# Activation, weight and table transposes of an SSM/MLP training step moved between the DMA queue and TensorE

## The chip, the core and the metric

One core of a Trainium2 chip runs the whole program: TensorE (PE) does the matmuls, VectorE (DVE), ScalarE (ACT) and GpSimd (POOL) the rest, and SyncE (SP) issues most of the DMAs. The metric is the device time of one execution in microseconds; lower is better. Engines run in parallel and each takes its own instructions in order, so an instruction that waits holds up everything behind it on its engine; the same is true of the transfers on one issuing queue.

## The reference, cut to what matters

The program computes a forward pass of four residual layers and the gradients of all their inputs. S = 2048 tokens, D = 512 features, F = 1376 hidden features, all in bf16.

```python
x = A_q
x = x + A(layernorm(x))      # A: q * (causal long convolution of kv with ssm_k + kv * ssm_D),
x = x + B(layernorm(x))      #    kv = shift_conv(k) * v
x = x + A(layernorm(x))
x = x + B(layernorm(x))      # B: gelu(x @ w1 + b1) @ w2 + b2
out, vjp = jax.vjp(f, A_q, A_k, A_v, A_shift_k, A_ssm_k, A_ssm_D, B_w1, B_b1, B_w2, B_b2)
return out, *vjp(grad_out)
```

The convolution's input does not depend on x, so it is done once (`y`) and both A layers use it. Backward, the gradient of y is the sum over both A layers (`gy_bf`), and one backward convolution follows. The weight gradients of w1 and w2 each sum over both B layers and all 2048 tokens: dw2 = h^T G, dw1 = (n^T gz), with h the gelu's output, G the gradient entering the layer, n the layer's normalised input and gz the gradient before the gelu. The gradient of b2 is the column sum of G over both layers.

## The kernel before

The program runs in stages. **Conv forward** (`phase_conv_forward`) makes sine tables (`tabN` for the filter, `tabF` and `tabI` for the data), shifts k, transforms filter and kv as matmuls over five frequency groups (`GROUPS`; `Fold.streams` prepares each group's input on DVE, `fwd_group` does the matmuls into `sp_ps`, `product` multiplies spectra on DVE, `inv_group` transforms back into `iv_ps`, `InvBlocks` combines on DVE). **MLP forward** and **MLP backward** (`phase_mlp`) cut the 2048 tokens into four slices of 512, each a lane (`fwd(s)`, `bwd(s)`); `interleave` emits the lanes in steps by a clock of rough costs, and the engines then run that order. A slice's input of a B layer is laid feature-major by DMA transposes on SP (`turn`, tiles `nT_sl` and, backward, `gT_sl`). The F features are handled as NFC = 11 chunks of 128 rows, the last with 96 rows and 32 of zeros. Backward, `b_bwd` needs w2 and w1 transposed (`w2T_sb`, `w1T_sb`); w1T has its mean over D removed (`centre_weights`, on DVE). h, gz and the gelu's derivative gp go to DRAM feature-major (`h_d`, `gz_d`, `gp_d`).

**Conv backward with weight gradients** is the last stage. `weight_grads` goes over 44 units (which weight, which layer, which chunk of 128 hidden features); a unit is 16 matmuls of 128x512 (`dw_ps<-G,dw_tm`), whose stationary operand `dw_tm` is h or gz with tokens on the partitions. That tile is fetched from `h_d` or `gz_d` by one DMA transpose on SP, five units ahead, in six buffers. The units' matmuls are the filler of the backward convolution: `conv_backward` yields numbers of microseconds at places where it expects PE to wait, and the top function puts that much filler there. PE's instructions are kept in that written order (`Ordered(nc, tc, ("tensor",))`); the other engines' orders are the scheduler's, by its own estimate of times. A finished sum goes from PSUM to SBUF on ACT (`dw_o`); for w1 it is also turned by four small matmuls (`dw_pt`, then `dw_oT` on ACT). Stores of results are issued on SP between the transposes (`flush`).

The backward convolution folds `gy_bf` on DVE (`fold_x`, `fold_s`, `fold_d`, `fold_t`), transforms it (`sp_ps` into `GY` on ACT), multiplies with the filter's spectrum (`Hb`, loaded on POOL's queue), transforms back, and makes the gradients of v, k and the shift filter. The filter's own gradient comes at the end (`cb_gh`): a table `tabG` of cosines and sines is built by POOL (`tg_u`), DVE and ACT, the spectra `GY` are multiplied in place with the data's spectrum (`KVb`, loaded on POOL's queue), and `gh_ps<-tabG,GY` are the last transforms.

The gradient of the output is loaded as `G` on SP at the end of the forward pass; out_0 and out_1 are stored half directly and half through a scratch copy in DRAM (`o0B`, `o1B`) that is reversed by `unflip_rows`.

## Time and profile before

| what | value |
|---|---|
| time, median of 3 runs (lowest to highest) | 1090.27 us (1090.2 to 1091.58) |
| profiled execution's own time | 1091.36 us |
| span of that execution in the profile | 1089.6 us |
| matmuls counted | 3856 |
| mean granted PE clock over the span | 0.87 of full speed |
| DMA traffic | 176.29 MB |

The profile gives, for one execution, how long each engine was busy, what ended its idle time, and which transfers were issued when. A matmul's own duration is its latency; matmuls follow one another faster than that, so the time of a row of n matmuls in the timeline, divided by n, is the cost of one. The granted clock scales it. Line numbers (L…) in rows of before are those of the listing above; L55 is a helper through which the ordered instructions go.

### The profile page before, as it was taken

The numbers are of one execution on the slowest core, as the hardware profiler recorded it, in microseconds if no ns is written. First come the engines' busy times: TensorE is split into PE (matmuls) and PEld (weight loads), VectorE is DVE, ScalarE is ACT, GpSimd is POOL, SyncE is SP. The second block draws the span as 40 slices with busy tenths as digits, with TensorE's granted clock in tenths as the row PEclk, the third lists the DMA queues.
The fourth block names the chain that finished last, engine by engine and source line by source line (L and its number), as shares of the span: only waits on it lengthen the run. The fifth ranks groups of instructions, "written<-read, shape, count | busy, mean of one in ns | idle before, by whom it ended". The sixth has DMA issues, their size and how long they took to land. (4 is left out here: it accounts for less than half of the span.)

```text
span 1089.6 us, 11131 instructions
## 1 busy us (share of the span) xinstructions
PE 785.0 (72%) x3856; PEld 359.2 (33%) x3917; DVE 728.8 (67%) x1373; ACT 468.8 (43%) x611; POOL 161.9 (15%) x281
## 2 busy tenths in 40 slices
...
GB/s 212 1 327 196 137 259 116 0 134 135 153 158 165 150 159 190 184 189 206 218 212 244 185 164 126 92 112 193 81 204 170 177 284 184 218 149 168 122 68 29
DMA packets 250979, 176.29 MB, mean 162 GB/s; under 512 B 152807, under 2 KB 238506, under 8 KB 250282
## 3 DMA queue, kind: packets, MB, share of 16 engines
...
q10 hardware_dynamic: 528, 0.00, 0.0%
...
## 5 line engine op out<-in xcount | busy, mean ns | idle before, releaser
L55 PE MATMUL dw_ps<-G,dw_tm 128*128 128x512 bf16 x687 | 171.5, 409 | 43.7 <-DMA dw_tm<-h_d 42.8
L957 PE MATMUL o_ps<-w_sb,h_sl 128*128 128x512 bf16 x345 | 96.0, 420 | 34.2 <-DVE h_sl L926 33.5
L55 PEld LDWEIGHTS <-dw_tm 128*128 128x128 bf16 x704 | 72.6, 105 | 135.5 <-DMA dw_tm<-h_d 41.5
L976 PE MATMUL gh_ps<-gT_sl,w2T_sb 128*128 128x512 bf16 x344 | 83.2, 390 | 29.6 <-DMA gT_sl<-G 26.6
L944 PE MATMUL z_ps<-nT_sl,w_sb 128*128 128x512 bf16 x345 | 82.6, 391 | 18.9 <-DMA nT_sl<-n_sl 18.1
L1032 ACT ACTIVATE nb_sl<-nb_sl,ab_ab 128x512 bf16<-128x512 bf16 x32 | 23.4, 802 | 159.4 <-DVE bb_junk L990 106.0
L987 PE MATMUL gn_ps<-w1T_sb,gz_sl 128*128 128x512 bf16 x345 | 83.3, 385 | 0.4
L1103 ACT ACTIVATE dw_o<-dw_ps 128x512 bf16<-128x512 f32 x22 | 13.1, 596 | 130.7 <-PE dw_ps L55 91.7
L978 DVE SCALAR_TENSOR_TENSOR gz_sl<-gh_ps,gpb 128x512 bf16<-128x512 f32 x88 | 58.5, 689 | 12.6 <-PE gh_ps L976 12.0
L946 ACT ACTIVATE g_z<-z_ps,b1col 128x512 bf16<-128x512 f32 x88 | 54.8, 694 | 19.9 <-PE z_ps L944 17.5
L957 PEld LDWEIGHTS <-h_sl 128*128 128x128 bf16 x352 | 34.0, 105 | 86.2 <-DVE h_sl L926 40.7
L976 PEld LDWEIGHTS <-w2T_sb 128*128 128x128 bf16 x352 | 35.1, 100 | 72.9 <-issue 34.8
L944 PEld LDWEIGHTS <-w_sb 128*128 128x128 bf16 x352 | 34.7, 100 | 64.7 <-DMA nT_sl<-n_sl 17.7
L987 PEld LDWEIGHTS <-gz_sl 128*128 128x128 bf16 x352 | 34.8, 99 | 40.7 <-issue 2.2
L869 POOL TENSOR_SCALAR rstd<-ln_mv 128x4 f32<-128x4 f32 x16 | 11.5, 719 | 236.2 <-DVE ln_mv L867 153.0
L922 ACT ACTIVATE g_s<-g_t 128x2048 bf16<-128x2048 bf16 (+1 forms) x24 | 42.5, 1773 | 8.9 <-DVE g_t L921 8.9
L993 POOL TENSOR_SCALAR bb_diag<-ident,bb_cols 128x128 bf16<-128x128 bf16 x32 | 17.0, 530 | 182.7 <-DVE bb_junk L990 181.8
L866 DVE BATCH_NORM_STATS2 ln_st<-x_sl 128x6 f32<-128x512 bf16 x64 | 41.9, 669 | 2.8 <-DMA x_sl<-in_A_q_dram 2.7
L919 ACT ACTIVATE g_q<-g_z 128x2048 bf16<-128x2048 bf16 (+1 forms) x24 | 42.9, 1788 | 0.1
L923 ACT ACTIVATE g_o<-g_t 128x2048 bf16<-128x2048 bf16 (+1 forms) x24 | 42.4, 1768 | 0.0
L880 ACT ACTIVATE n_sl<-x_sl,ln_nmr,rstd 128x512 bf16<-128x512 bf16 x32 | 24.7, 820 | 37.3 <-POOL ln_nmr L873 37.3
L55 PE MATMUL sp_ps<-fold_t,tabN 128*128 128x512 bf16 x85 | 30.2, 460 | 12.4 <-DVE fold_t L55 12.2
...
## 6 DMA issues: line engine op xcount, KB each, us to landing
n_d<-n_sl SPq DMA_DIRECT2D x16, 512.0 KB, 3.4
h_d<-h_sl SPq DMA_DIRECT2D x16, 512.0 KB, 2.9
gp_d<-g_p SPq DMA_DIRECT2D x16, 512.0 KB, 3.3
nb_sl<-n_d SPq DMA_DIRECT2D x16, 512.0 KB, 4.3
gpb<-gp_d SPq DMA_DIRECT2D x16, 512.0 KB, 5.0
gz_d<-gz_sl SPq DMA_DIRECT2D x16, 512.0 KB, 4.2
Hspec_d<-Hg SPq DMA_DIRECT2D x8, 512.0 KB, 4.1
...
```

The lines of the kernel that those rows point to most:

```text
L55: return self.tc.keep_in_program_order(f(*args, **kwargs))
L866: nc.vector.bn_stats(out=st, in_=x[:, t, :])
L880: nc.scalar.activation(out=n[:, t, :], in_=x[:, t, :], func=ACT.Identity, bias=nmr[:, t:t + 1], scale=rstd[:, t:t + 1])
L919: nc.scalar.activation(out=q, in_=zb, func=ACT.Square)
L922: nc.scalar.activation(out=sg, in_=t, func=ACT.Sigmoid)
L923: nc.scalar.activation(out=o, in_=t, func=ACT.Sigmoid, scale=-1.0)
L944: nc.tensor.matmul(ps, lhsT=w.w1[:, dc, c * P:(c + 1) * P], rhs=nT[:, dc, :], start=(dc == 0), stop=(dc == ND - 1))
L946: nc.scalar.activation(out=zb[:, c - c0, :], in_=ps, func=ACT.Identity, bias=w.b1col[:, c:c + 1])
L957: nc.tensor.matmul(ps, lhsT=h[:, c, t * P:(t + 1) * P], rhs=w.w2[:, c, :], start=False, stop=(c == NFC - 1))
L976: nc.tensor.matmul(ps, lhsT=w.w2T[:, dc, c * P:(c + 1) * P], rhs=gT[:, dc, :], start=(dc == 0), stop=(dc == ND - 1))
L978: nc.vector.scalar_tensor_tensor(out=gz[:, c, :], in0=ps, scalar=1.0, in1=gp[:, c - c0, :], op0=ALU.mult, op1=ALU.mult, accum_out=m.b1part ...
L987: nc.tensor.matmul(ps, lhsT=gz[:, c, t * P:(t + 1) * P], rhs=w.w1T[:, c, :], start=(c == 0), stop=(c == NFC - 1))
```

## The change

Seven edits, all in one step:

1. **Weight-gradient operands.** `dw_tm` is no longer fetched by a DMA transpose. A plain load on SP brings h or gz feature-major (`dw_fm`, four buffers, fetched four units ahead), 16 transposes on PE per unit turn it in two halves of eight into PSUM (`dw_tp`, two buffers), and ACT copies each half (128x1024) to `dw_tm` (three buffers). The halves of unit k+1 are placed after the matmuls 2 and 9 of unit k. The `dw_pt` matmuls of a finished w1 chunk move to matmul 5 of the next unit, the stores to matmul 12, and SP's order is kept as written for this part. `G` is reloaded in four pieces.
2. **Weights.** `w2T` and `w1T` are made on PE right after the forward convolution: 44 transposes and 8 copies for w2T; for w1T, 44 matmuls of 512 columns with a constant that subtracts the mean, 44 of 128 columns with the identity, and 11 copies on ACT. The DMA transposes and `centre_weights` go.
3. **The table of the filter's gradient.** `tabG` is turned out of `tabN` by 64 transposes on PE and 8 copies on ACT in the forward convolution, kept in DRAM (`tabG_d`) and loaded on POOL's queue where it was built before. Its 257th column is made apart (`col256`).
4. **b2.** The first of the 32 zero rows of the last chunk of w2 holds b2/16, and the bias of the matching hidden feature is 16, so that h there is 16: the matmul that added b2 (`o_ps<-b2row`) and the matmuls that summed G for its gradient (`db_ps`) go, and the gradient is a row of the last dw2 sum.
5. **Start of the backward pass.** `gT_sl` of the last layer is transposed straight from DRAM (grad_out and its flipped copy) and `G` and `nb_sl` are loaded after the slice's first group.
6. **Convolution backward.** `gy_bf` is left by the MLP backward already folded once (sums and differences of token pairs of a slice), so `fold_x` goes; `fold_d` is computed when group 2 asks for it. The product with `KVb` moves from the end into the loop over groups, behind `inv_group`. `unflip_rows` go on POOL's queue. `gk_o` shares buffers with `vb`.
7. **Pools** of these stages reuse memory tile by tile (`reuse_waits="tile"`): a new tile waits for the old tiles at its place, not for all of the closed pool.

SyncE at the end of the forward pass: x_sl is a slice's output, gpb the gelu's derivative loaded for the backward pass, gT_sl and G the incoming gradient. Before:

```order
L949 DMA h_d<-h_sl 128x3x512
L209 DMA out_dram<-x_sl 128x2x512
L950 DMA gp_d<-g_p 128x3x512
L55 DMA_TRANSPOSE w2T_sb<-w_sb 128x4x128
L209 DMA o0B_d<-x_sl 128x2x512
L55 DMA_TRANSPOSE w2T_sb<-w_sb 128x4x128
L55 DMA_TRANSPOSE w1T_sb<-w_sb 128x11x128 x4
L972 DMA gpb<-gp_d 128x4x512 x2
L211 DMA G_3677<-in_grad_out_dram 128x2x512
L211 DMA G_3677<-goB_d 128x2x512
```

After:

```order
L221 DMA out_dram<-x_sl 128x2x512
L926 DMA_TRANSPOSE gT_sl<-in_grad_out_dram 128x4x128 x2
L926 DMA_TRANSPOSE gT_sl<-goB_d 128x4x128 x2
L975 DMA h_d<-h_sl 128x4x512
L221 DMA o0B_d<-x_sl 128x2x512
L976 DMA gp_d<-g_p 128x4x512
L975 DMA h_d<-h_sl 128x3x512
L221 DMA out_dram<-x_sl 128x2x512
L976 DMA gp_d<-g_p 128x3x512
L221 DMA o0B_d<-x_sl 128x2x512
L995 DMA gpb<-gp_d 128x4x512
L223 DMA G_3864<-in_grad_out_dram 128x2x512
```

The transposes of the weights are gone from the queue, the transposes of gT_sl now read grad_out and its flipped copy and stand ahead of the last stores of the forward pass, and the loads of G follow the first gpb load instead of standing ahead of the first gT_sl.

SyncE at the end of the MLP backward and the start of the last stage: nb_sl holds the gradient of the first input here, o1B_d its half stored in scratch. Before:

```order
L1008 DMA nb_sl<-n_d 128x4x512
L209 DMA out_dram<-nb_sl 128x2x512
L209 DMA o1B_d<-nb_sl 128x2x512
L1065 DMA_TRANSPOSE dw_tm<-h_d 128x16x128 x2
L1186 DMA out_dram<-b1o 128x10x1
L1189 DMA out_dram<-b1o 96x1
L1065 DMA_TRANSPOSE dw_tm<-h_d 128x16x128
L209 DMA out_dram<-nb_sl 128x2x512
L209 DMA o1B_d<-nb_sl 128x2x512
L1065 DMA_TRANSPOSE dw_tm<-h_d 128x16x128
L199 DMA out_dram<-o1B_d 4x256x512
L1065 DMA_TRANSPOSE dw_tm<-h_d 128x16x128 x2
```

After:

```order
L221 DMA out_dram<-nb_sl 128x2x512
L221 DMA o1B_d<-nb_sl 128x2x512
L1100 DMA dw_fm<-h_d 128x2048
L55 DMA dw_fm<-h_d 128x2048
L1245 DMA out_dram<-b1o 128x10x1
L1248 DMA out_dram<-b1o 96x1
L55 DMA dw_fm<-h_d 128x2048
L221 DMA out_dram<-nb_sl 128x2x512
L221 DMA o1B_d<-nb_sl 128x2x512
L55 DMA dw_fm<-h_d 128x2048
L55 DMA out_dram<-dw_o 128x512
L55 DMA dw_fm<-h_d 128x2048 x2
```

Each fetch is now a plain load of 128x2048 instead of a transpose, six loads stand ahead of the last two nb_sl stores (three of them above this piece) where three transposes stood, and the reversal of o1B is not on this queue any more.

GpSimd at the end of the convolution's backward pass: tg_u are the arguments of the table, KVb the data's spectrum. Before:

```order
L690 DMA kTc<-kT_d 128x2176 x2
L685 DMA out_dram<-gk_o 128x4x512 x2
L738 DMA KVb<-KVspec_d 128x2x1024 x2
L711 IOTA qrow_i 128x272
L716 IOTA kcol_i 128x2 x2
L716 IOTA kcol_i 128x4 x3
L731 IOTA nyq_i 1x272
L713 CAST qrow<-qrow_i 128x272
L718 CAST kcol<-kcol_i 128x16
L723 TENSOR_SCALAR tg_u<-qrow,kcol 128x272 x12
L738 DMA KVb<-KVspec_d 128x2x2048
L723 TENSOR_SCALAR tg_u<-qrow,kcol 128x272 x8
```

After, the same place:

```order
L221 DMA o3B_d<-ksb_b 128x2x512
L211 DMA out_dram<-o3B_d 4x256x512
L713 DMA out_dram<-gk_o 128x4x512 x2
L718 DMA kTc<-kT_d 128x2176 x2
L713 DMA out_dram<-gk_o 128x4x512 x2
L739 DMA tabG<-tabG_d 128x16x256 x2
L740 COPY tabG<-col_80 128x32
L747 IOTA nyq_i 1x272
L791 DMA out_dram<-gh 128x2048 x4
L793 DMA out_dram<-gdo 128x4x1
```

The computation of tg_u is gone and two loads of the table stand in its place; the loads of KVb stand earlier, each behind the load of Hb of its group (not shown).

The diff, cut to its core:

```diff
-        unflip_rows(nc, aps["out_0"].flatten_outer_dims(), dram.o0B)
-        unflip_rows(nc, aps["out_1"].flatten_outer_dims(), dram.o1B)
...
-            nc = Ordered(nc, tc, ("tensor",))
-            fill = weight_grads(nc, m, dims, aps, dw)
+            conv_nc = Ordered(nc, tc, ("tensor",))
+            fill = weight_grads(Ordered(nc, tc, ("tensor", "sync")), m, dims, aps, dw)
...
 
 
+def turn_integer_table(nc, psum, pool, consts, tabN, dest):
+
+    for f in range(2):
+        for k0 in (0, 8):
+            tg = pool.tile([P, 8, 2, P], BF16, name="tg", tag="kn", bufs=4)
+            for qt in range(2):
+                ps = psum.tile([P, 8, P], BF16, name="tn_ps", tag="kt", bufs=2)
+                for k in range(8):
+                    nc.tensor.transpose(out=ps[:, k, :], in_=tabN[:, f, qt, (k0 + k) * P:(k0 + k + 1) * P],
+                                        identity=consts.ident)
+                nc.scalar.activation(out=tg[:, :, qt, :], in_=ps, func=ACT.Identity)
+            nc.gpsimd.dma_start(out=dest[:, f, k0:k0 + 8, :].rearrange("p k (t q) -> p k t q", t=2), in_=tg)
+
...
+        if k1 == 2:
+            tt(out=D, in0=X[:, :, 0:2], in1=X[:, :, 2:4], op=ALU.subtract)
...
+    turn_integer_table(nc, psum, gp, consts, tabN, dram.tabG)
...
-        gyv = res.gy_bf[:, :, :].rearrange("p (i h) d -> p i (h d)", i=4)
-        fg = Fold(nc, tp, gyv[:, :, 0:2 * D], gyv[:, :, 2 * D:4 * D], False)
-        yield 24.0
+        fg = Fold(nc, tp, None, None, False, res.gy_bf[:, :, :].rearrange("p (i e h) d -> p e i (h d)", i=4, e=2))
+        yield 28.0
...
+    unflip_rows(nc, aps["out_0"].flatten_outer_dims(), dram.o0B, eng=nc.gpsimd)
+    unflip_rows(nc, aps["out_1"].flatten_outer_dims(), dram.o1B, eng=nc.gpsimd)
...
                 inv_group(nc, psum, tabI, Y, g, W)
+                KV = gyp.tile([P, 2, 4, 512], BF16, name="KVb", tag="Sg", bufs=2)
+                dma(out=KV[:, :, 0:n, :], in_=dram.KVspec[:, :, base:base + n, :])
+                Rb = spec_second(nc, rot, KV) if g == 0 else None
+                product(nc, rot, GY[g], KV, Rb, g, GY[g], True)
+                yield 4.0
...
-                nc.vector.tensor_single_scalar(out=u, in_=u, scalar=8191, op=ALU.bitwise_and)
-                nc.scalar.activation(out=tabG[:, f, k0:k0 + 4, :], in_=u, func=ACT.Sin, scale=SIN_SCALE,
-                                     bias=consts.pibias)
+            dma(out=tabG[:, f, :, 0:256], in_=dram.tabG[:, f])
+        nc.gpsimd.tensor_copy(out=tabG[:, :, :, 256], in_=consts.col256)
...
-        for g, (k1, base, n) in enumerate(GROUPS):
-            KV = gyp.tile([P, 2, 4, 512], BF16, name="KVb", tag="Sg", bufs=2)
-            dma(out=KV[:, :, 0:n, :], in_=dram.KVspec[:, :, base:base + n, :])
-            Rb = spec_second(nc, hp, KV) if g == 0 else None
-            product(nc, hp, GY[g], KV, Rb, g, GY[g], True)
-            yield 1.3 * n
...
+    nc.gpsimd.memset(b1t[pad:pad + 1, nfull:nfull + 1], PAD_H)
+    nc.sync.dma_start(out=w.w2[pad:pad + 1, nfull, :], in_=aps["B_b2"].rearrange("(o d) -> o d", o=1))
+    nc.vector.tensor_scalar(out=w.w2[pad:pad + 1, nfull, :], in0=w.w2[pad:pad + 1, nfull, :], scalar1=1.0 / PAD_H,
+                            scalar2=None, op0=ALU.mult)
...
+    for dc in range(ND):
+        for c0 in (0, 8):
+            k = min(8, NFC - c0)
+            ps = psum.tile([P, 8, P], BF16, name="w2_ps", tag="mm", bufs=4)
+            for c in range(k):
+                nc.tensor.transpose(out=ps[:, c, :], in_=w.w2[:, c0 + c, dc * P:(dc + 1) * P], identity=consts.ident)
+            nc.scalar.activation(out=w.w2T[:, dc, c0 * P:(c0 + k) * P], in_=ps[:, 0:k, :], func=ACT.Identity)
     for c in range(NFC):
-        order.sync.dma_start_transpose(out=w.w2T[:, :, c * P:(c + 1) * P], in_=w.w2[:, c, :])
-        yield 8.0
...
+        ps = psum.tile([P, D], F32, name="w1_ps", tag="oo", bufs=4)
+        cs = slice(c * P, (c + 1) * P)
+        for dc in range(ND):
+            nc.tensor.matmul(ps, lhsT=w.w1[:, dc, cs], rhs=w.centre, start=(dc == 0), stop=(dc == ND - 1))
+        for dc in range(ND):
+            nc.tensor.matmul(ps[:, dc * P:(dc + 1) * P], lhsT=w.w1[:, dc, cs], rhs=consts.ident, start=False,
+                             stop=True, skip_group_check=True)
+        nc.scalar.activation(out=w.w1T[:, c, :], in_=ps, func=ACT.Identity)
...
-        nc.sync.dma_start_transpose(out=dst[:, :, t * P:(t + 1) * P], in_=src[:, t, :])
+        nc.sync.dma_start_transpose(out=dst[:, :, t * P:(t + 1) * P], in_=src[t])
...
-        nc.tensor.matmul(ps, lhsT=w.ones_row, rhs=w.b2row, start=False, stop=False)
...
+        if c0 == 0:
+            if load:
+                load()
+            n = m.spool.tile([P, TS, D], BF16, name="nb_sl", tag="n", bufs=m.n_bufs)
+            nc.sync.dma_start(out=n, in_=tok(m.n_d[l], s))
...
-        nc.vector.tensor_tensor(out=m.gy[:, sl, :], in0=m.gy[:, sl, :], in1=p, op=ALU.add)
+        nc.vector.tensor_tensor(out=p, in0=m.gy[:, sl, :], in1=p, op=ALU.add)
+        for e, op in enumerate((ALU.add, ALU.subtract)):
+            nc.vector.tensor_tensor(out=m.gy[:, s * TS + 2 * e:s * TS + 2 * e + 2, :], in0=p[:, 0:2, :], in1=p[:, 2:4, :],
+                                    op=op)
...
+    d.evp = stack.enter_context(tc.tile_pool(name="dw_ev", bufs=3, reuse_waits="tile"))
+    d.tp = stack.enter_context(tc.tile_pool(name="dw_tm", bufs=1, reuse_waits="tile"))
+    d.pp = stack.enter_context(tc.tile_pool(name="dw_ps", bufs=2, space=bass.MemoryType.PSUM, reuse_waits="tile"))
...
-    def fetch(k):
+    fms, tms, pss, turned, late = {}, {}, {}, [], []
+
+    def fetch(k, sync):
+        if k >= len(units):
+            return
         which, i, c = units[k]
-        tms[k] = d.tp.tile([P, NT, P], BF16, name="dw_tm", tag=f"dw_tm{i}")
-        nc.sync.dma_start_transpose(out=tms[k], in_=(m.gz_d if which else m.h_d)[layers[i]][:, c, :])
+        pool = d.evp if k % 4 == 3 else d.tp
+        fms[k] = pool.tile([P, S], BF16, name="dw_fm", tag=f"dw_fm{k % 4}", bufs=1)
+        sync.dma_start(out=fms[k], in_=(m.gz_d if which else m.h_d)[layers[i]][:, c, :])
+
+    def turn_half(k, half):
+        if k >= len(units):
+            return
+        if half == 0:
+            tms[k] = (d.evp if k % 3 == 2 else d.tp).tile([P, NT, P], BF16, name="dw_tm", tag=f"dw_tm{k % 3}", bufs=1)
+        ps = d.pp.tile([P, 8, P], BF16, name="dw_tp", tag="dw_tp")
+        for j in range(8):
+            t = 8 * half + j
+            nc.tensor.transpose(out=ps[:, j, :], in_=fms[k][:, t * P:(t + 1) * P], identity=m.ident)
+        dst = tms[k][:, 8 * half:8 * half + 8, :]
+        nc.scalar.activation(out=dst, in_=ps, func=ACT.Identity)
+
...
-    for k in range(ahead):
-        fetch(k)
-    psb = d.pp.tile([1, D], F32, name="db2_ps", tag="dw_ps")
-    for i in range(2):
-        for t in range(NT):
...
+    def reload(x, l):
+        for s in range(4):
+            nc.sync.dma_start(out=m.G[x][:, s * TS:(s + 1) * TS, :], in_=tok(m.n_d[l], s))
+
+    for k in range(4):
+        fetch(k, nc.nc.sync)
+    for half in range(2):
+        turn_half(0, half)
+        yield 0.45
     for k, (which, i, c) in enumerate(units):
-        if k + ahead < len(units):
-            fetch(k + ahead)
-        flush()
-        if which == 1 and (k == 0 or units[k - 1][0] == 0):
-            nc.sync.dma_start(out=m.G[1], in_=m.n_d[1].rearrange("(t p) d -> p t d", p=P))
+        if which == 1 and units[k - 1][0] == 0:
+            reload(1, 1)
+        fetch(k + 4, nc.sync)
         f0, fcs = dims.FC[c]
         if i == 0:
             pss[c] = d.pp.tile([P, D], F32, name="dw_ps", tag="dw_ps")
         ps, tm = pss[c], tms.pop(k)
         for t in range(NT):
+            if t in (2, 9):
+                turn_half(k + 1, int(t == 9))
+                yield 0.45
+            if t == 5:
+                turn_out()
+            if t == 12:
+                flush()
             nc.tensor.matmul(ps, lhsT=tm[:, t, :], rhs=m.G[i][:, t, :], start=(i == 0 and t == 0),
                              stop=(i == 1 and t == NT - 1))
             yield 0.23
...
+            turned.append((o, f0, fcs))
+    turn_out()
     flush()
...
+            turn_weights(nc, m.psum, m.w, wback, consts, dims)
...
+                g3 = G3[:, s * TS:(s + 1) * TS, :]
+                yield from b_bwd(nc, m, g3, 3, s, ret, dram_rows(go_ap, dram.goB, s),
+                                 lambda: tok_io(nc, g3, go_ap, dram.goB, s))
```

153 lines of the change are left out of this document (67 added, 86 removed).

## The prediction

> **What bounds the kernel now.** I first read the table of engine times by stage, cut where the work changes: conv forward, MLP forward, the passage to the backward pass, MLP backward, and the last stage in two pieces.
>
> ```profile
> core 0: us, PE busy (x) PEld busy (x) DVE busy (x) ACT busy (x) POOL busy (x), PEclk, DMA share, GB/s
> 0.00:220.00 220.00, 141.02 (x820) 69.70 (x829) 131.98 (x225) 103.25 (x134) 34.48 (x65) 0.84 0.43 155
> 220.00:480.00 260.00, 192.81 (x753) 74.86 (x768) 227.97 (x344) 211.63 (x224) 40.58 (x64) 0.87 0.54 161
> 480.00:506.00 26.00, 0.46 (x2) 0.14 (x2) 11.06 (x34) 6.46 (x10) 0.00 (x0) 0.60 1.03 252
> 506.00:698.00 192.00, 168.37 (x721) 70.98 (x735) 151.51 (x428) 37.33 (x52) 24.06 (x60) 0.96 0.64 180
> 698.00:760.00 62.00, 28.22 (x97) 10.51 (x98) 25.12 (x37) 4.87 (x8) 4.11 (x7) 0.69 0.75 134
> 760.00:1078.00 318.00, 254.10 (x1467) 133.03 (x1485) 181.14 (x307) 104.94 (x186) 58.67 (x85) 0.91 0.74 160
> ```
>
> No engine bounds the whole. DVE bounds MLP forward (228 of 260 us), PE MLP backward (168 of 192). In two places nothing computes: 480 to 506 and 698 to 760, and there the DMA share is highest (1.03 and 0.75). The last stage, 698 to 1078, is 380 us in which PE is busy 282. The list of waits of that stage says for whom:
>
> ```profile
> PE dw_ps L55 <- DMA dw_tm<-h_d: 42.8, 5, 15.7
> ACT dw_o L1103 <- DMA out_dram<-dw_o: 30.9, 2, 16.5
> PE dw_pt L55 <- ACT dw_o L1103: 27.4, 11, 9.2
> DVE fold_x L221 <- DMA o1B_d<-nb_sl: 23.8, 1, 23.8
> PE gt_ps L55 <- ACT gksT L670: 17.4, 8, 15.2
> ```
>
> PE's three rows make 42.8 + 27.4 + 17.4 = 87.6 us. The first is the transposed operand itself. The third begins with the second row: ACT stands 16.5 us at a dw_o whose buffer's store is not out, and the gksT copies behind it wait too. The timeline of PE and of SP's queue at the stage's start shows how:
>
> ```profile
> 714.78 4.91 PE L55 MATMUL dw_ps<-G,dw_tm 128*128 128x512 bf16 x22
> 735.44 9.98 PE L55 MATMUL dw_ps<-G,dw_tm 128*128 128x512 bf16 x31 [15.75 <-DMA dw_tm<-h_d]
> 759.17 3.41 PE L55 MATMUL dw_ps<-G,dw_tm 128*128 128x512 bf16 x9 [13.75 <-DMA dw_tm<-h_d]
> 762.42 1.89 PE L55 MATMUL sp_ps<-fold_t,tabFb 128*128 128x512 bf16 x8
> ...
> 712.57 10.27 SPq L1065 DMA_TRANSPOSE dw_tm<-h_d  x1
> 726.84 2.17 SPq L209 DMA_DIRECT2D o1B_d<-nb_sl  x1
> 737.57 21.33 SPq L1065 DMA_TRANSPOSE dw_tm<-h_d  x2
> ```
>
> One transpose holds SP for 10.27 us, two for 21.33. The o1B_d store comes behind the first, so its buffer is late for fold_x (the 23.8 us row), and sp_ps stands behind the dw_ps that wait. A matmul of 512 columns costs 4.91 / 22 = 0.223 us on a busy PE, but 9.98 / 31 = 0.322 after a wait: a long wait costs some 3 us more, as the granted clock (0.69 here, 0.91 later) confirms.
>
> **The change, part by part.** The sum is made against the profiled execution: 1091.36 us, of which the span is 1089.6; it lies 1.1 above the median of 1090.27.
>
> *Last stage.* The cost of transposes on PE comes from the ones before has in its prologue (three rows of PE's timeline, and the copies), and from 128-column matmuls that wait for nothing:
>
> ```profile
> 129.23 1.07 PE L55 MATMUL tt_ps<-ident,tabF 128*128 128x128 bf16 x16
> 134.75 1.93 PE L55 MATMUL tt_ps<-ident,tabF 128*128 128x128 bf16 x16 [4.45 <-ACT tabI L185]
> 136.87 3.72 PE L55 MATMUL tt_ps<-ident,tabF 128*128 128x128 bf16 x32 [0.20 <-ACT tabI L185]
> 926.66 9.10 PE L55 MATMUL gk_ps<-wdiag_b,gksT 128*128 128x128 bf16 x160
> ...
> L185 ACT ACTIVATE tabI<-tt_ps x4: 1017/1020/1024, 133.7 to 136.7; 128x1024 bf16<-128x1024 bf16 x4
> ...
> L55 PE MATMUL db_ps<-G,onescol x32: 379/379/634, 699.0 to 708.0; 128*1 128x512 bf16 x32
> ```
>
> 44 units x 16 = 704 transposes at 9.10 / 160 = 0.057 us are 40 us of PE; the upper bound is the prologue's pace, from 129.23 to 140.59, 11.36 / 64 = 0.178 us, 125 us in all. I take the lower one: between two halves lie seven matmuls of 0.223 us, 1.56 us, in which the 1.02 us copy fits, and there are two PSUM buffers. ACT gains 88 x 1.02 = 90 us; it was busy 110 of 380, and loses the table's sines. The db_ps go (some 9 us, 699.0 to 708.0). What the moves should buy is the waits: plain loads in place of transposes take away the 42.8 and the late stores behind them (15.2 of the 17.4, the 23.8 of fold_x, which itself is dropped). The dw_pt rows (27.4) go twice over: they move behind five matmuls of the next unit, and the table no longer puts ACT into POOL's pace. So of the 380: 380 - 88 = 292, less 9, plus 40, is 323 us. Less the slow matmuls after long waits, eight of them at 3.1, is 298. New waits come in: KVb shares its two buffers with Hb, so that each load starts later, and each half of PSUM waits for ACT. The next rows are for these, the loads in this stage and the two queues there (packets, MB, share of all DMA time):
>
> ```profile
> Hb<-Hspec_d POOLq DMA_DIRECT2D x3, 1024.0 KB, 14.2
> q1 hardware_dynamic: 106006, 32.09, 49.3%
> q0 software_dynamic: 7296, 26.89, 24.8%
> ```
>
> New waits are not in the trace: from 0 to the old 88. I take 20, one Hb landing of 14.2 and six for the rest, because the queue that carries the transposes (q1) pays 49.3 / 32.09 = 1.54% per MB against 0.92% on the other, so that Hb should land sooner than it did. Stage: 318, that is **-62** (-26 to -82).
>
> *Passage to the backward pass* (SP's queue, PE, DVE):
>
> ```profile
> 482.48 0.53 SPq L209 DMA_DIRECT2D o0B_d<-x_sl  x1
> 484.33 6.60 SPq L55 DMA_TRANSPOSE w1T_sb<-w_sb  x4
> 490.97 1.35 SPq L972 DMA_DIRECT2D gpb<-gp_d  x2
> 498.35 5.17 SPq L909 DMA_TRANSPOSE gT_sl<-G  x4
> 505.72 6.63 PE L976 MATMUL gh_ps<-gT_sl,w2T_sb 128*128 128x512 bf16 x21 [25.54 <-DMA gT_sl<-G]
> 507.62 0.69 DVE L978 SCALAR_TENSOR_TENSOR gz_sl<-gh_ps,gpb 128x512 bf16<-128x512 f32 x1 [4.01 <-PE gh_ps L976]
> ...
> gpb<-gp_d SPq DMA_DIRECT2D x16, 512.0 KB, 5.0
> ```
>
> w1T's transposes, G and gT_sl leave the chain; the last output's store stays ahead of gpb, so gpb is issued near 482.5 (where the last store is now), lands 5.0 later, and the first gz_sl comes near 487.5 instead of 507.6: **-20**. What is late next is gpb. Lower bound of the gain 12, if the eight gT_sl transposes that now stand ahead of the last stores hold SP for another 8 us (5.17 for four); upper 22.
>
> *MLP backward.* The pre-fold adds two half passes per slice. The nearest row is a whole pass:
>
> ```profile
> 701.13 1.22 DVE L1017 TENSOR_TENSOR ab_p<-nb_sl,g_sl 128x2048 bf16<-128x2048 bf16 x1
> ```
>
> Four slices at 1.22 to 2.44 are 5 to 10 us of DVE, beside a PE that is the bound; only the last slice's lies open: **+2** (0 to +10).
>
> *MLP forward and weights.* The 32 matmuls of b2row go, 32 x 0.223 = 7 us of PE in a stage that DVE bounds: **-3** (-7 to 0). The weights' 88 matmuls of 128 and 44 of 512 columns stand in an idle PE and ACT:
>
> ```profile
> 231.77 0.59 PE L954 MATMUL o_ps<-x_sl,ident 128*128 128x512 bf16 x1 [31.46 <-DVE x_sl L903]
> 237.12 2.93 ACT L880 ACTIVATE n_sl<-x_sl,ln_nmr,rstd 128x512 bf16<-128x512 bf16 x4 [35.70 <-POOL ln_nmr L873]
> 103.97 0.61 PE L55 MATMUL sp_ps<-fold_t,tabN 128*128 128x512 bf16 x1 [4.84 <-DVE fold_t L55]
> ```
>
> On a slow PE they take 88 x 0.116 (3.72 / 32) + 44 x 0.322 = 24 us, inside 31.46; ACT's 19 copies at most 19 us, inside 35.70: **0** (if the cover is gone, +24).
>
> *Conv forward.* 64 transposes are 7.4 us at that pace, and 4.84 of PE's wait at 103.97 covers most: **+3** (0 to +8).
>
> Sum: -62 - 20 + 2 - 3 + 0 + 3 = -80. Span 1010, execution 1011, median **1010**.
>
> **The rivals.**
>
> *Transfers stay late (1046).* The loads move as many bytes as the transposes did, over DMA engines that were busy 0.74 of the last stage, with POOL's 26.89 MB beside them. If half of the 88 us returns as waits for dw_fm, Hb and KVb, with half of the slow matmuls, the stage is 298 + 12 + 44 = 354: -26, sum -44. For it: POOL's queue gets two more loads and two reversals, and Hb took 14.2 us. Against: q1's price per MB, and SP held 10 to 21 us by transposes alone. [...] The two queue rows speak against it, though they hold other transfers too.
>
> *No new wait (985).* Stage 298, passage -22, prologue 0: -82 - 22 - 3 + 2 = -105. For it, a stretch of the stage that ran nearly so:
>
> ```profile
> 780.00:860.00 80.00, 75.63 (x333) 33.66 (x338) 51.09 (x72) 24.64 (x32) 8.66 (x13) 0.96 0.83 157
> ```
>
> Against: PE follows one written order, filled by guesses of how long the convolution waits.
>
> *The passage gains nothing (1030).* If the G loads or gpb behind them land as late as before, the -20 is lost. Against: gT_sl no longer reads G.
>
> *ACT sets PE's pace (1101, slower).* Place: each dw_tp half. If PE stands until ACT has copied, at the prologue's 1.42 us per eight (11.36 / 8) instead of 0.46, 88 halves cost 85 more, the clock stays low, and the stage is 323 + 85 = 408, +28; with -18 elsewhere +10. It decides from 75 / 88 = 0.85 us per half on. For it: ACT is in order, and its row of 30.9 shows that it can stand. Against: the prologue's last 32 took 0.93 per eight with nothing between the halves. [...]
>
> **How the numbers follow.** Forecast 0.50, late transfers 0.24, no new wait 0.13, no gain in the passage 0.06, ACT's pace 0.07. From 978 to 1052 lie nearly all of the first and fourth, four fifths of the second and half of the third: 0.8. The forecast's own range is 995 to 1028. About 0.2% (2 us) is what a measurement can tell from no change: faster 0.91, same 0.03 (the upper end of late transfers), slower 0.06.
>
> **What would show it.** Right: PE's wait for its first gh_ps under 8 us and the first gz_sl near 487; no wait of dw_ps for a transfer over 5 us; sp_ps starting under 40 us after the last MLP backward matmuls instead of 64 (762.42 less 698); the last stage some 318 us at a clock of 0.95. Wrong: dw_tp waiting for ACT in total over 30 us; product rows waiting for Hb or KVb; gh_ps waiting for tabG; w1T's matmuls pushing the first z_ps past 246.

## The result and the profile after

The changed kernel takes 1017.74 us (four executions, 1014.58 to 1019.7) against 1090.92 us of the kernel before, run beside it (four, 1090.2 to 1093.6): a ratio of 0.9322, 95% interval 0.9293 to 0.9351. Measured again later it took 1022.32 us (six, 1018.95 to 1024.64), ratio 0.9367 (0.9329 to 0.9404), so two measurements of one kernel can lie 0.5% apart. Ratios leave out executions that lie over 1.5% above the fastest of their kernel, which matters below for two of the kernels with transposing loads; differences between kernels of different chips are therefore taken from the ratios.

First the table of engine times by stage, cut where the work changes (the first three rows are the forward pass and the passage to the backward pass, the fourth the MLP backward, the last two the last stage up to the convolution's first transform and from there):

```profile
core 0: us, PE busy (x) PEld busy (x) DVE busy (x) ACT busy (x) POOL busy (x), PEclk, DMA share, GB/s
0.00:208.00 208.00, 143.49 (x880) 74.81 (x890) 113.70 (x191) 109.01 (x140) 37.74 (x90) 0.87 0.48 174
208.00:254.00 46.00, 19.98 (x141) 11.04 (x142) 38.26 (x79) 15.95 (x26) 5.14 (x12) 0.73 0.30 87
254.00:489.70 235.70, 181.19 (x733) 75.90 (x747) 209.70 (x301) 209.55 (x222) 35.95 (x52) 0.90 0.56 163
489.70:688.50 198.80, 164.08 (x707) 69.81 (x722) 153.70 (x432) 42.41 (x59) 30.83 (x61) 0.95 0.69 197
688.50:731.00 42.50, 30.98 (x204) 17.03 (x205) 22.47 (x38) 18.75 (x22) 6.64 (x9) 0.90 0.70 184
731.00:1009.00 278.00, 263.14 (x2016) 159.35 (x2049) 171.08 (x299) 167.79 (x252) 33.72 (x47) 1.00 0.59 187
```

In the last stage (688.5 to 1009) PE is busy 31.0 + 263.1 = 294.1 of 320.5 us, at a full clock from 731 on. Before it was busy 28.2 + 254.1 = 282.3 of 380. So the stage has 11.8 us more of PE's work and 97.7 - 26.4 = 71.3 us less idle time: -59.5. For the comparison the stages are cut at these rows of the timeline, the last matmuls of the conv forward, of the MLP forward and of the MLP backward. Before (the row of the first gz_sl stands in the prediction):

```profile
195.83 4.48 PE L55 MATMUL iv_ps<-Yg,tabI 128*128 128x512 bf16 x20
477.42 2.76 PE L957 MATMUL o_ps<-w_sb,h_sl 128*128 128x512 bf16 x12 [0.76 <-DVE h_sl L926]
696.20 1.71 PE L995 MATMUL gn_ps<-nb_sl,bb_diag 128*128 128x512 bf16 x3 [6.27 <-DVE bb_junk L990]
1077.77 0.60 ACT L1111 ACTIVATE dw_oT<-dw_pt 128x512 bf16<-128x512 f32 x1 [0.54 <-PE dw_pt L55]
```

And after, with the first gz_sl, the first sp_ps of the last stage and the last store of the convolution:

```profile
203.31 5.87 PE L55 MATMUL iv_ps<-Yg,tabI 128*128 128x512 bf16 x22 [0.22 <-issue]
485.89 2.76 PE L982 MATMUL o_ps<-w_sb,h_sl 128*128 128x512 bf16 x12 [0.30 <-DVE h_sl L952]
494.53 0.69 DVE L1001 SCALAR_TENSOR_TENSOR gz_sl<-gh_ps,gpb 128x512 bf16<-128x512 f32 x1 [5.34 <-DMA gpb<-gp_d]
686.81 1.72 PE L1023 MATMUL gn_ps<-nb_sl,bb_diag 128*128 128x512 bf16 x3 [7.00 <-DVE bb_junk L1018]
731.33 1.90 PE L55 MATMUL sp_ps<-fold_t,tabFb 128*128 128x512 bf16 x8 [2.03 <-DMA tabFb<-tabF_d]
977.22 0.76 POOL L793 DMA_DIRECT2D out_dram<-gdo  x1
1008.96 0.60 ACT L1120 ACTIVATE dw_oT<-dw_pt 128x512 bf16<-128x512 f32 x1 [0.49 <-PE dw_pt L55]
```

Start plus duration of these rows gives the end of each stage (for the first gz_sl its start counts). Forecast and measured differences:

| stage, ending at | before, us | after, us | difference | forecast |
|---|---|---|---|---|
| conv forward, last iv_ps | 200.3 | 209.2 | +8.9 | +3 |
| MLP forward with the weights, last o_ps | 279.9 | 279.5 | -0.4 | -3 |
| passage, first gz_sl | 27.4 | 5.9 | -21.5 | -20 |
| MLP backward, last gn_ps | 190.3 | 194.0 | +3.7 | +2 |
| last stage, last dw_oT | 380.5 | 321.0 | -59.5 | -62 |
| tail, end of the span | 11.2 | 3.2 | -8.0 | none |
| span | 1089.6 | 1012.8 | -76.8 | -80 |

The waits of the last stage, in which before's rows began with 42.8 for dw_tm:

```profile
ACT dw_tm L1112 <- PE dw_tp L55: 70.4, 74, 7.1
PE dw_tp L55 <- DMA dw_fm<-h_d: 7.8, 2, 6.1
PE gt_ps L55 <- ACT gksT L698: 3.6, 8, 1.2
PE dw_ps L55 <- ACT dw_tm L1112: 1.9, 3, 1.2
```

ACT waits for PE's transposes 70 us, PE for ACT's copies 1.9 us in all. The groups of the stage's transposes and copies:

```profile
L55 PE MATMUL dw_tp<-ident,dw_fm 128*128 128x128 bf16 x704 | 55.2, 223 | 7.8 <-DMA dw_fm<-h_d 7.8
L1112 ACT ACTIVATE dw_tm<-dw_tp 128x1024 bf16<-128x1024 bf16 x88 | 89.8, 1023 | 74.8 <-PE dw_tp L55 70.4 <-DVE bb_junk L1049 4.0 <-remote 0.3
```

The queues (packets, MB, share of all DMA time) and the loads (KB each, us to land):

```profile
q1 hardware_dynamic: 19986, 29.47, 34.2%
q0 software_dynamic: 8880, 30.04, 26.5%
Hb<-Hspec_d POOLq DMA_DIRECT2D x3, 1024.0 KB, 5.6
tabFb<-tabF_d POOLq DMA_DIRECT2D x1, 2048.0 KB, 24.2
out_dram<-o1B_d POOLq DMA_DIRECT2D x1, 1024.0 KB, 23.3
```

SP's queue moves 29.47 MB in 19,986 packets where it was 32.09 MB in 106,006, and a megabyte costs 34.2 / 29.47 = 1.16% of the stage's DMA time instead of 1.54%. As the windows differ in length (319 and 380 us), that is 3.7 us of all 16 DMA engines for a megabyte instead of 5.8. Hb lands in 5.6 us instead of 14.2, but tabFb in 24.2 where it took 11.1 before.

### The profile page after: what moved, and what is told of

Its sections match the earlier page's. It is cut to its first block, busy times and chain, and to the rows that moved or that the text cites. A ratio compares the mean times of both kernels' runs of the same rounds, so it can differ in the third digit from the quotient of the medians.

```text
span 1012.8 us, 12851 instructions
## 1 busy us (share of the span) xinstructions
PE 802.9 (79%) x4675; PEld 408.0 (40%) x4753; DVE 708.9 (70%) x1337; ACT 564.0 (56%) x718; POOL 150.0 (15%) x271
## 4 chain that ended last, share of the span: by engine, by line
PE 22%; DVE 21%; DMA 13%; ACT 9%; issue 7%; POOL 4%; SPq 2%; POOLq 0%; DVEq 0%; another core or an unknown queue 0%; ACTq 0%
PE dw_ps L55 7%; PE gh_ps L999 4%; DVE ln_st L883 2%; DMA tabFb<-tabF_d 2%; DMA gpb<-gp_d 2%; PE gh_ps L55 2%; PE sp_ps L55 2%; DMA nb_sl<-n_d 2%; PE dw_tp L55 2%; DVE g_o L953 2%; DMA ksb_b<-ks_d 2%; ACT g_o L949 2%; ACT g_z L972 2%; ACT g_s L948 2%; DVE gz_sl L1001 2%
## 5 line engine op out<-in xcount | busy, mean ns | idle before, releaser
L55 PE MATMUL dw_ps<-G,dw_tm 128*128 128x512 bf16 x671 | 166.3, 383 | 3.5 <-ACT dw_tm L1112 1.9
L1112 ACT ACTIVATE dw_tm<-dw_tp 128x1024 bf16<-128x1024 bf16 x88 | 89.8, 1023 | 74.8 <-PE dw_tp L55 70.4
L55 PEld LDWEIGHTS <-dw_tm 128*128 128x128 bf16 x704 | 65.3, 99 | 63.1 <-ACT dw_tm L1112 3.0
L1015 PE MATMUL gn_ps<-w1T_sb,gz_sl 128*128 128x512 bf16 x344 | 80.6, 379 | 1.3 <-DVE g_sl L1024 0.9
L1001 DVE SCALAR_TENSOR_TENSOR gz_sl<-gh_ps,gpb 128x512 bf16<-128x512 f32 x88 | 58.2, 688 | 25.6 <-DMA gpb<-gp_d 16.1
L982 PEld LDWEIGHTS <-h_sl 128*128 128x128 bf16 x352 | 36.5, 107 | 93.0 <-DVE h_sl L952 45.1
L55 PE MATMUL dw_tp<-ident,dw_fm 128*128 128x128 bf16 x704 | 55.2, 223 | 7.8 <-DMA dw_fm<-h_d 7.8
L55 PEld LDWEIGHTS <-dw_fm 128*128 128x128 bf16 x704 | 48.0, 100 | 29.3 <-DMA dw_fm<-h_d 8.7
L999 PEld LDWEIGHTS <-w2T_sb 128*128 128x128 bf16 x352 | 35.3, 101 | 59.5 <-issue 21.2
L945 ACT ACTIVATE g_q<-g_z 128x2048 bf16<-128x2048 bf16 (+1 forms) x24 | 42.8, 1783 | 0.1
L1039 ACT ACTIVATE ab_u<-y_res,onescol_f,rstd 128x512 bf16<-128x512 bf16 x32 | 23.3, 802 | 29.4 <-DVE G L1062 22.9
```

The source lines that it names most:

```text
L55: return self.tc.keep_in_program_order(f(*args, **kwargs))
L945: nc.scalar.activation(out=q, in_=zb, func=ACT.Square)
L982: nc.tensor.matmul(ps, lhsT=h[:, c, t * P:(t + 1) * P], rhs=w.w2[:, c, :], start=False, stop=(c == NFC - 1))
L999: nc.tensor.matmul(ps, lhsT=w.w2T[:, dc, c * P:(c + 1) * P], rhs=gT[:, dc, :], start=(dc == 0), stop=(dc == ND - 1))
L1001: nc.vector.scalar_tensor_tensor(out=gz[:, c, :], in0=ps, scalar=1.0, in1=gp[:, c - c0, :], op0=ALU.mult, op1=ALU.mult, accum_out=m.b1part ...
L1015: nc.tensor.matmul(ps, lhsT=gz[:, c, t * P:(t + 1) * P], rhs=w.w1T[:, c, :], start=(c == 0), stop=(c == NFC - 1))
```

## The experiments

Edit numbers are those of the section on the change; all kernels but the second are edits of the changed kernel.

**Edit 1 undone: transposing loads again, everything else kept.** The operand comes from a DMA transpose, six buffers, five units ahead.

```diff
-        fms[k] = pool.tile([P, S], BF16, name="dw_fm", tag=f"dw_fm{k % 4}", bufs=1)
-        sync.dma_start(out=fms[k], in_=(m.gz_d if which else m.h_d)[layers[i]][:, c, :])
+        tms[k] = pool.tile([P, NT, P], BF16, name="dw_tm", tag=f"dw_tm{k % 6}", bufs=1)
+        sync.dma_start_transpose(out=tms[k], in_=(m.gz_d if which else m.h_d)[layers[i]][:, c, :])
...
-                turn_half(k + 1, int(t == 9))
```

> The changed kernel (1017.7 us), with only the way of the weight-gradient operand put back: dw_tm comes by DMA transposes on SP again, five units ahead in six buffers; no transposes and no copies of it on PE and ACT. All other edits stay. My theory is that the transposes' delay was what the last stage lost: of PE's old waits the 42.8 us for dw_tm and the 15.2 us behind late dw_o stores return, and 40 us of PE transposes go, but PE then idles in their place; the last stage, 321 us now, becomes 340 to 355, the whole 1035 to 1050. Rival: the other edits of that stage (dw_pt moved, table loaded, product moved, pools, reversals off SP) brought the gain, and the PE transposes only cost their 40 us; then the stage falls to about 285 and the whole to 980.

Measured: 1064.15 us, ratio 0.973 (0.9684 to 0.9775). That is 0.036 to 0.041 above the change, 40 to 44 us: above the theory's range, and far from the rival's. The kernel has 704 transposes and 88 copies less and is slower. How much of this belongs to the reversals, which the change puts beside these loads, is asked further below.

**Edit 1 alone, put into the kernel before.** Plain loads, transposes on PE, moved dw_pt and SP's written order for this part, in the old pools' places (dw_ev with two buffers, for room; the three pools of the weight gradients reuse memory tile by tile, so a part of edit 7 comes along).

```diff
-        nc.sync.dma_start_transpose(out=tms[k], in_=(m.gz_d if which else m.h_d)[layers[i]][:, c, :])
+        fms[k] = pool.tile([P, S], BF16, name="dw_fm", tag=f"dw_fm{k % 4}", bufs=1)
+        sync.dma_start(out=fms[k], in_=(m.gz_d if which else m.h_d)[layers[i]][:, c, :])
...
+                turn_half(k + 1, int(t == 9))
```

> The kernel before (1090.9 us) with only the way of the weight-gradient operand changed: plain loads, transposes on PE, copies on ACT, dw_pt behind five matmuls of the next unit, stores behind twelve, SP's order as written there. The sums for b2's gradient, the table built by POOL, the order of products and the pools of the convolution stay as before. My theory: waits of 42.8 + 15.2 us and the 23.8 us of fold_x go, 40 us of PE come, so some 40 to 50 us are won, 1040 to 1050. Rival, that this edit needs the others (the table's sines in ACT's order hold up the copies, the reversals hold up SP): below 15 us won, 1075 or more.

Measured: 1067.27 us, ratio 0.978 (0.9742 to 0.9819), 24 us faster than before; between the two expectations, so both missed. Its last stage is 363.8 us, 16.7 less than before; its tail is 3.2 us instead of 11.2. The waits in its last stage:

```profile
DVE fold_x L221 <- DMA dw_fm<-h_d: 18.5, 1, 18.5
PE dw_ps L55 <- ACT dw_tm L1081: 17.1, 4, 7.8
ACT tabG L726 <- DVE tg_u L725: 14.9, 7, 4.0
PE dw_tp L55 <- DMA dw_fm<-h_d: 10.3, 2, 6.3
```

PE's waits for the operand's transfers fall from 42.8 us to 10.3, and waits for ACT's copies come in: 15.5 of these 17.1 us lie between 890 and 960, where ACT makes the table and waits for DVE. So ACT stands there in the table's pace, set by POOL and DVE; fold_x still waits behind the stage's loads. The operand is worth 24 us alone and 40 to 44 with the other edits, the reversals on POOL's queue among them.

**Edit 3 undone: the table built by POOL, DVE and ACT at the end** (no turning in the conv forward; gh with two buffers, for room).

```diff
-    turn_integer_table(nc, psum, gp, consts, tabN, dram.tabG)
...
-            dma(out=tabG[:, f, :, 0:256], in_=dram.tabG[:, f])
+            for k0 in range(0, 16, 4):
+                u = hp.tile([P, 4, NQP], I32, name="tg_u", tag="tg_u", bufs=2)
```

> The changed kernel with only the table of the filter's gradient put back: built by POOL, DVE and ACT in the last stage, and not turned out of tabN in the forward convolution (the filter gradient's result tiles have two buffers instead of four, to make room). In the trace of the change the forward convolution ends 8.9 us later than before and the 64 transposes stand in it from 99.5 to 108.8 where before had a gap of 4.8. If that edit costs the prologue its time and the chain at the end has slack (the filter's gradient is done 32 us before the end), this is 4 to 8 us faster, 1010 to 1014. Rival: POOL's 26 us chain puts ACT and with it the dw_tm copies behind it, PE stalls for 10 to 20 us in the last stage, and this is slower, 1022 to 1032.

Measured: 1027.21 us, ratio 0.9397 (0.9355 to 0.944); this is the rival's range, not the expected gain. By the ratios it is 3 to 8 us slower than the two measurements of the change, and its interval overlaps that of the second. The profile, of the longest of the four executions, splits it: the last stage is 338.2 us (+17.2), the conv forward ends at 206.0 (-3.2). Two of PE's waits in the last stage:

```profile
PE gh_ps L55 <- ACT tabG L748: 5.3, 1, 5.3
PE dw_tp L55 <- ACT dw_tm L1121: 4.2, 1, 4.2
```

The table on ACT delays both the last transforms and the operand's copies. These rows are 9.5 of the 17.2 us; the rest is open.

**The operand turned twice.** Each half is transposed and copied twice, so the same result costs 704 transposes and 88 copies more; the filler that a half counts for is doubled with it.

```diff
+        ps = d.pp.tile([P, 8, P], BF16, name="dw_tp", tag="dw_tp")
+        for j in range(8):
+            t = 8 * half + j
+            nc.tensor.transpose(out=ps[:, j, :], in_=fms[k][:, t * P:(t + 1) * P], identity=m.ident)
+        nc.scalar.activation(out=dst, in_=ps, func=ACT.Identity)
```

> The changed kernel with every half unit of the weight-gradient operand turned and copied twice, into the same place: 704 more transposes on PE (40 us at 0.057) and 88 more copies on ACT (90 us at 1.02). If a transpose costs only its own PE time, as the sum took it, the whole is 40 to 46 us longer, 1058 to 1064. Rival: ACT's copies set PE's pace (two PSUM buffers now serve twice the halves); then a second copy costs its own 1.02 us and the whole is 75 to 95 us longer, 1093 to 1113.

Measured: 1065.35 us, ratio 0.977 (0.9735 to 0.9804), just above the theory's range and far from the rival's. The last stage is 370.7 us, 49.7 longer: 49.7 / 704 = 0.071 us per transpose, copies and waits included, 0.56 per half. ACT as the pace, 1.02 us per half, would have cost 90. Both copies in its last stage, and what ACT waits for:

```profile
L1112 ACT ACTIVATE dw_tm<-dw_tp 128x1024 bf16<-128x1024 bf16 x88 | 90.1, 1024 | 36.3 <-PE dw_tp L55 33.2 <-remote 2.9
L1117 ACT ACTIVATE dw_tm<-dw_tp 128x1024 bf16<-128x1024 bf16 x88 | 90.1, 1023 | 2.9 <-PE dw_tp L55 0.2
```

Even with twice the copies ACT stands 33 us waiting for PE.

**Edit 5 undone: gT from G.** G is loaded ahead of the backward pass and gT_sl transposed out of it.

```diff
+        for i in range(NSL):
+            tok_io(nc, G3[:, i * TS:(i + 1) * TS, :], go_ap, dram.goB, i)
...
-                yield from b_bwd(nc, m, g3, 3, s, ret, dram_rows(go_ap, dram.goB, s),
-                                 lambda: tok_io(nc, g3, go_ap, dram.goB, s))
+                yield from b_bwd(nc, m, g3, 3, s, ret, sb_rows(g3))
```

> The changed kernel with the start of the backward pass put back in one point: G is loaded ahead of it, and the last layer's gT_sl is transposed from G again and not from DRAM; the weights stay turned on PE. The passage to the first gz_sl shrank from 25.1 to 4.9 us. If the chain load of G, transpose, first gh_ps brought half of it, the whole is 9 to 14 us longer, 1027 to 1032. Rival: the w1T transposes and their centring were the whole chain, and loading G hides behind the gpb loads that now come last; then the whole is within 4 us of 1017.7.

Measured: 1032.86 us, ratio 0.9444 (0.9409 to 0.9479), just above the theory's range. The passage is 26.3 us again, and the wait is the old one; with it, the transposes on SP's queue:

```profile
PE gh_ps L999 <- DMA gT_sl<-G: 24.4, 1, 24.4
496.24 13.20 SPq L926 DMA_TRANSPOSE gT_sl<-G  x4
```

Before, these four held SP 5.17 us. Here the reversal of out_0 runs beside them, issued on POOL's queue at 493.4, so some 8 of the 20 us that come back may be the reversal's and not the order's of G and gT_sl.

The MLP backward behind it is 187.2 instead of 194.0, so 7 of the 20 are won again there: with the late start gz_sl no longer waits for gpb.

**Start of the conv forward mended.** fold_d computed early as before, the scaling of b2 on POOL, the table turned in two parts.

```diff
+        if integer:
+            tt(out=self.D, in0=X[:, :, 0:2], in1=X[:, :, 2:4], op=ALU.subtract)
...
-    nc.vector.tensor_scalar(out=w.w2[pad:pad + 1, nfull, :], in0=w.w2[pad:pad + 1, nfull, :], scalar1=1.0 / PAD_H,
+    nc.gpsimd.tensor_scalar(out=w.w2[pad:pad + 1, nfull, :], in0=w.w2[pad:pad + 1, nfull, :], scalar1=1.0 / PAD_H,
```

> The changed kernel with three orders of the forward convolution mended: the filter's fold_d is computed at once as before and not when group 2 asks, b2's scaling is done by POOL and not in DVE's order (DVE waited 3.7 us for b2's load), and the table is turned in two halves, one after group 2 and one after group 3 of the filter. The forward convolution is 8.9 us longer in the change than before. If these three placements cost it, 5 to 8 us come back, 1009 to 1013. Rival: the 9 us are the work itself (64 transposes and 8 copies on an ACT that is busy there); then at most 2 us come back.

Measured: 1017.1 us, ratio 0.9311 (0.9274 to 0.9349), no gain; its last iv_ps ends at 210.3. The places that I had taken for the cause of the slower start are not it.

**The reversals of out_0 and out_1 late.** They go from POOL's queue, at the start of the last stage in program order, to SP's, behind units 30 and 34.

```diff
-    unflip_rows(nc, aps["out_0"].flatten_outer_dims(), dram.o0B, eng=nc.gpsimd)
-    unflip_rows(nc, aps["out_1"].flatten_outer_dims(), dram.o1B, eng=nc.gpsimd)
...
+                if k == 30:
+                    unflip_rows(nc, aps["out_0"].flatten_outer_dims(), dram.o0B)
+                if k == 34:
+                    unflip_rows(nc, aps["out_1"].flatten_outer_dims(), dram.o1B)
```

> The changed kernel with the two reversals of out_0 and out_1 (1 MB each, DRAM to DRAM) put on SP late in the last stage, behind the units 30 and 34, in place of POOL's queue, where out_0's is issued at 493.5 while the first gz_sl wait 16 us for gpb. If the reversal takes the loads' bandwidth there, the waits for gpb fall to under 7 us and 4 to 8 us are won, 1010 to 1014. Rival: gpb is late by its own order on SP and buffers; then nothing changes there, 1016 to 1019.

Measured: 1011.22 us (1009.14 to 1013.75), ratio 0.9251 (0.9218 to 0.9284): the fastest kernel here, and its interval lies below both of the change's. The cause lies at the start of the MLP backward. In the changed kernel the 1 MB reversal of o0B starts on POOL's queue just as SP issues the loads of gpb (timeline of POOL and of SP's queue), and takes 19.1 us to land:

```profile
493.54 1.73 POOL L211 DMA_DIRECT2D out_dram<-o0B_d  x1 [66.15 <-DMA o0B_d<-x_sl]
490.16 0.61 SPq L995 DMA_DIRECT2D gpb<-gp_d  x1
501.83 6.12 SPq L995 DMA_DIRECT2D gpb<-gp_d  x1
```

The waits there, from 475 to 520 us, are DVE for gpb and PE behind DVE:

```profile
DVE gz_sl L1001 <- DMA gpb<-gp_d: 16.1, 4, 9.2
PE gh_ps L999 <- DVE gz_sl L1001: 11.5, 2, 6.6
```

With the reversal late, in that kernel's waits from 470 to 530:

```profile
DVE gz_sl L999 <- DMA gpb<-gp_d: 6.5, 2, 5.5
PE gh_ps L997 <- DVE gz_sl L999: 6.8, 1, 6.8
```

The MLP backward falls from 194.0 to 184.8 us. The last stage grows by 3.5, from 321.0 to 324.5: there the two reversals now run on SP's queue, and the plain load right behind each of them holds SP 9.7 and 8.0 us, where most hold it for 0.3.

**Whole pools.** Edit 7 undone: `reuse_waits="tile"` is taken out of the 11 pools to which the change gave it.

> The changed kernel without tile-by-tile reuse of memory in the pools of the weights, the weight gradients and the backward convolution (each new pool waits for all of the closed ones at its place). The transposes on PE alone won 24 us on the kernel before, where I expected 40 to 50, and there fold_x waited 18.5 us. If the pools are what the operand needed beside it, this is 12 to 25 us longer, 1030 to 1043. Rival: the other edits (table, products) made the difference; then 1016 to 1022.

Measured: 1036.82 us, ratio 0.9487 (0.9455 to 0.9518), as expected; the last stage is 339.8 us (+18.8). Three waits of it, one of each engine, show what a whole pool holds up:

```profile
POOL tabFb L632 <- ACT dw_tm L1112: 13.5, 1, 13.5
DVE fold_s L239 <- DMA o1B_d<-nb_sl: 14.9, 1, 14.9
PE gh_ps L55 <- DMA tabG<-tabG_d: 13.0, 2, 10.6
```

**Transposing loads, all three reversals late on SP.** The first experiment with the reversals of out_0, out_1 and out_3 behind units 30, 34 and 38, so that the transposes at the start of the last stage have no reversal beside them.

> The changed kernel with the operand fetched by DMA transposes again (as in the first run of that name, 1064 us) and with all three reversals (out_0, out_1, out_3, each 1 MB from DRAM to DRAM in rows of 1 KB) on SP late in the last stage, behind units 30, 34 and 38. In that first run the transposes took SP 2.3 us each before 703 and 7 to 18 us each between 704 and 772, while the reversal of out_1 and POOL's loads of 6 MB ran. If the reversals are what slows the transposes, the 20 us waits of dw_ps go and 20 to 35 us are won, 1030 to 1044. Rival: POOL's plain loads slow them as well; then at most 8 us are won, 1056 or more.

Measured: ratio 0.9465 (0.9406 to 0.9523), median 1044.26 over executions from 1031.49 to 1054.86. Against the first experiment some 29 us are won by the ratios, 20 by the medians: about half or more of what the transposing loads cost there was the reversals beside them. Against the kernel with two late reversals and transposes on PE (0.9251) this one is slower by 23 us by the ratios and 33 by the medians; that is nearer to what the way of the operand is worth with the reversals out of the way. What stays is seen at its start, in the timeline of SP's queue, in the times of its first five transposes (ns, lowest, median and highest) and in SP's waits from 690 to 790:

```profile
699.00 10.92 SPq L1097 DMA_TRANSPOSE dw_tm<-h_d  x1
753.11 25.11 SPq L55 DMA_TRANSPOSE dw_tm<-h_d  x2
L1097 SPq DMA_TRANSPOSE dw_tm<-h_d x5: 2145/2509/11802, 693.1 to 727.8; - x5
SPq L55 <- PE dw_ps L55: 28.4, 5, 19.5
```

PE's wait for them in the last stage:

```profile
PE dw_ps L55 <- DMA dw_tm<-h_d: 33.7, 5, 15.1
```

Two of the first five transposes hold SP for 10.9 and 11.8 us, though no reversal runs; the other three take 2.1 to 2.5. A row of the timeline can also hold a wait between two transfers: the 25.11 us at 753 are 5.6 us of two transposes and 19.5 us in which SP waits for PE's dw_ps, which frees the buffer. Beside the slow ones POOL loads Hb, KVb and tabFb, issued between 700 and 702; that these loads are the cause is argued from their place and was not tried by moving them. PE's two long waits differ: the one of 15.1 us ends when the transpose of 10.9 has landed, but another of 14.6 ends already at 697.7, at the first operand. SP issued that one only at 693.1, where the changed kernel issues its first plain load at 675.9. So a part of what the transposing loads cost here is a late start and not their pace; why they start late is open.

**The same with less filler per yield.** In the kernel just shown PE ran out of weight gradients at 999 us and waited for the convolution; here each number that the convolution yields is taken three quarters.

```diff
-                room += slack
+                room += 0.75 * slack
```

> The kernel of the run with the DMA operand and late reversals (1044 us, spread 1031 to 1055), with the filler that each pause of the convolution asks for cut to 0.75, since without the PE transposes the filler ran out at 999 us there, 15 us before the convolution's last work, and its end at 1029 was the convolution's store. If PE's transposes are not needed once the reversals are away and the filler fits, this comes within 10 us of the change, 1015 to 1028. Rival: the DMA transposes still starve dw_ps at the start, and the cut filler only moves the waits; then it stays at 1035 to 1050.

Measured: 1045.3 us, ratio 0.957 (0.9526 to 0.9615); the last stage is 352.0 us. It does not come near the change, 1022.32 on the same chip. PE's waits for the operand, of h and of gz:

```profile
PE dw_ps L55 <- DMA dw_tm<-h_d: 37.1, 6, 15.8
PE dw_ps L55 <- DMA dw_tm<-gz_d: 10.4, 1, 10.4
```

So less filler, at least in this measure, does not bring the transposing loads level.

**All three reversals late, first gpb on POOL's queue.** An attempt to gain on the fastest kernel.

```diff
-        nc.sync.dma_start(out=gp[:, 0:k, :], in_=m.gp_d[l][:, c0:c0 + k, s * 512:(s + 1) * 512])
+        (nc.gpsimd if l == 3 and s == 0 else nc.sync).dma_start(out=gp[:, 0:k, :], in_=m.gp_d[l][:, c0:c0 + k, s * 512:(s + 1) * 512])
```

> The changed kernel with all three reversals late on SP as in the run beside it (two of them alone won 6.5 us), and the first slice's three gpb loads of the backward pass issued on POOL's queue, which is idle there, and not behind the last stores on SP. If gpb's place on SP is what the first gz_sl still wait for (5.5 us), 2 to 5 us more are won, 1005 to 1010. Rival: gpb waits for its buffer, which the last gelu group holds; then 1010 to 1013.

Measured: 1025.22 us, ratio 0.9394 (0.9346 to 0.9443), not faster than the change; both expectations missed. The first gz_sl now waits for the store of what it loads, not for a queue:

```profile
DVE gz_sl L998 <- DMA gp_d<-g_p: 5.6, 1, 5.6
```

The last stage is 335.0 us: its transposes wait for `dw_fm` 9.2, 4.6 and 7.6 us. The last of these waits ends at 1003: the load behind the reversal of out_3 holds SP 15.4 us, and little work is left after unit 38 to cover it. The edit changed two things at once, so which of them lost the gain was not separated.

**The change once more**, for the spread between chips:

> The changed kernel itself, beside it on the same chip, as a measure of how far runs of one kernel on another chip and day go: 1014 to 1020 as first measured, if the chips agree within 0.3%.

Measured: 1022.32 us, ratio 0.9367; its stages are within about 1 us of the first profile except the conv forward, which ends at 214.3 instead of 209.2.

## Why the prediction was right, and where it was not

It forecast 1010 us and 978 to 1052; 1017.74 lies inside, and inside the forecast's own 995 to 1028. Step by step:

*Last stage, -62: measured -59.5.* The terms hold nearly. The price of a transpose, taken as 0.057 us from matmuls and bounded at 0.178 by the prologue, came out as 0.071 with copies and waits when the work was doubled. PE's work was to grow by 40 - 9 - 25 = 6 us and grew by 11.8; the 25 for slow matmuls were counted for eight long waits, a count that no row gives. The 87.6 us of waits for the operand, ACT's stores and gksT are gone, 3.6 of gksT and 1.9 of dw_pt left. Idle time of PE was to fall by 88 - 20 = 68 us and fell by 71.3. The signs: dw_ps waits 1.9 us in all for copies and for no load of an operand, but PE's transposes wait 7.8 for dw_fm, one of them 6.1; the clock is 0.90 and then 1.00, better than 0.95; sp_ps starts 731.3 - 688.5 = 42.8 us after the last MLP backward matmuls, just over the 40. There tabFb is late (24.2 us to land) and PE stands 2.0 us for it.

*What the sum did not say* is how its terms hang together. It read the 88 us as a list from which each edit strikes its rows. Edit 1 by itself took away 32.5 us of PE's waits for the operand's transfers, 17.7 at dw_pt and 14.7 at gt_ps, yet the stage gained only 16.7: some 40 us of transposes came in (704 at 0.057), and 17.1 us of waits for ACT's copies, most of them in the table's pace. Undoing the table costs 17.2 in the stage, undoing the tiled pools 18.8. The 363.8 of edit 1 alone less 17.2 and 18.8 is 327.8, and 321.0 is measured with everything, so these three carry most of it; that their prices add is argued here from single runs and was not tried in pairs. What an edit is worth also depends on the rest: the operand brought 24 us alone, 40 to 44 with reversals beside the transposing loads, and 23 to 33 with the reversals late.

*Late transfers (the rival of 1046)* came only in part: SP's queue got cheaper per MB, 1.16% for 1.54%, and Hb landed in 5.6 us, but tabFb in 24.2. The two queue rows pointed the right way. On the queue of this stage the transposing loads were the slower ones: with the reversals out of the way two transposes still hold SP 10.9 and 11.8 us, where a plain load of the operand in the changed kernel holds it 1.7 at most, and PE waits 15.1 us for the first of the two. In landing, the two kinds are nearer: 7.5 and 6.1 us (h and gz, medians of the kernel before) against 5.1 and 5.8. One reading of the prediction was too simple: SP was held "by transposes alone" for 10.27 us, but the row of 21.33 begins right behind the reversal of o1B, and it is the first of its two transposes that takes 19.0. Plain loads right behind a late reversal on SP are held in the same way, for 8.0 to 15.4 us.

*ACT as PE's pace (1101)* is refuted by the doubled work: 0.56 us per half, that is 0.071 us for one more transpose in a row of eight, copies and waits included, with ACT waiting for PE.

*Passage, -20: measured -21.5*, and undoing edit 5 brings 20 back, some 8 of them perhaps through the reversal beside. PE's longest wait at a gh_ps there is 6.6 us, under the 8 of the sign. The first gz_sl comes at 494.5, not 487, only because everything before it is 8.5 us later. The step named gpb as what is late next; it is, but the step did not see what makes it late: the reversal that the change moved to POOL's queue. The prediction noted those two reversals only as load on POOL's queue, under the last stage. The place where one of them costs is the MLP backward, +3.7 instead of +2; without it there the stage is 184.8, 5.5 less than before.

*Tail, not in the sum: -8.0.* Before, the convolution's last store, of gdo, was issued at the very end and took 14.7 us to land:

```profile
1072.37 0.77 POOL L783 DMA_DIRECT2D out_dram<-gdo  x1
```

And its row among the DMA issues:

```profile
out_dram<-gdo POOLq DMA_DIRECT2D x1, 1.0 KB, 14.7
```

After, it is issued at 977.2 and PE ends on weight gradients. The prediction took what lies behind the last dw_oT as fixed. Edit 1 alone moves it already (tail 3.2).

*Conv forward, +3: measured +8.9.* This term was mis-sized. The run without the table ends at 206.0, so about 3 us or more are the table's; kernels with it end between 208 and 214. Another part is spread: edit 1 alone leaves this stage as it was, and still its last iv_ps ends at 202.9, 2.6 later than before. What is left is open; fold_d's place, b2's scaling and the table's place are not it, by the run that mended them. *MLP forward, -3: measured -0.4.* The weights' transposes are hidden as forecast, since the stage is not longer. The first z_ps does come at 253.8, past the 246 that was named as a sign of being wrong, but only because the conv forward ends later: it starts 44.6 us behind it, where it was 45.7. The 7 us of b2row matmuls were worth nothing in a stage that DVE bounds, which was the upper bound given.

Measured less forecast, the stages are off by +5.9, +2.6, -1.5, +1.7, +2.5 and -8.0, together +3.2 us of span. That they cancel so well is luck: 12.7 us of terms that came out worse stand against 9.5, most of it the tail that no term held. The median lies 7.7 above 1010: these 3.2, another 3.2 because the profiled execution, 1014.58, is the fastest of the four, and 1.1 because before's profiled execution lay above its median. Edits 2, 4 and 6 were not tried alone; of edit 6 only the place of the reversals was.
